# Two stretches per head pair, logits weighed apart from values, and table stores issued behind relus

## The chip, the cores and the metric

The kernel runs on one NeuronCore of one Trainium2 chip. A core has five instruction queues: PE (TensorE, matrix products; its weight loads are shown as PEld), DVE (VectorE), ACT (ScalarE), POOL (GpSimd) and SP (SyncE, which here only issues transfers). They run side by side and wait for each other through semaphores. The time is the device time of one execution, in microseconds (us). Three runs of the kernel before took 858.88, 858.96 and 869.34 us, so its time is the median, 858.96. The profile is of one further execution, which took 851.99 us.

## The reference

```python
# attention: B=8 batches, 8 heads, S=576 tokens, head size 64
scores = scale * np.matmul(q, k.transpose(0, 1, 3, 2))
cum = np.cumsum(np.maximum(s, 0.0), axis=-1)
bias = -(cum[:, :, :, None] - cum[:, :, None, :])
scores = np.where(causal, -1000000000.0, scores + np.minimum(bias, 0.0))
...
attn = attn / (np.sum(attn, axis=-1, keepdims=True) + 1e-09)
x = np.matmul(attn, v)                      # then heads side by side: 512 wide
# experts: 8 of them, 512 -> 1024 -> 512
logits = np.einsum('bsd,de->bse', x, w_gate)
local_gate = 1.0 / (1.0 + np.exp(-np.einsum('bsd,de->bse', x, w_local).squeeze(-1)))
# token by token: the argmax expert if s == 0 or local_gate < 0.5, else the expert of the token before
h = np.maximum(x[b, s] @ w1[e], 0.0)
out[b, s] = p[e] * (h @ w2[e])
```

All in float32, 4608 tokens.

## The kernel before

**Attention** runs over 32 pairs of heads, n = 0 to 32 with b, hp = n // 4, n % 4 (loop at L893). The bias splits into a factor for the query, which drops out in the division by the sum, and one for the key. So the values are multiplied once per batch by the keys' weights (`weigh`, L770), and the exponential of the plain scores is multiplied with them. `scores(n, u)` (L784) makes the transposed score tile u of a pair: PE multiplies kb by qb (L796), ACT takes the exponential into `e` (L798) and POOL zeroes what lies above the diagonal (L782). Tiles 0, 1 and 2 are 1024 wide and share two PSUM buffers `ps_s`; tile 3 is the 64-token tail `et` (L805, L806). `values(n, j0, j1)` (L816) multiplies the exponentials of a pair by the weighed values `vg` and the tail `vt` (L831, L834), and DVE divides by the sum into `xb`, the rows of x (L837 to L841). Beside its 64 values each row of `vg` carries the logits of the router for its token (from `value_logits`, L748, which multiplies vT by the gate's weights and copies the result into `va` and `vl`) and a column of ones, all weighed together at L775 and L778. So the rows and the logits of x come out of one product.

The order is written out by hand: each engine runs its instructions in the order of the program. Pair n's tiles 0 and 1 come first, then the first six value blocks of pair n - 1, then tiles 2 and 3, then the other three value blocks. `load_v(b + 1)` at the start of each batch issues vT, va and vl on SP; vl takes two transfers (L661). `load_qk(n + 4)` asks for q and k four pairs ahead. At n = 0 there is no earlier pair; instead `key_weights`, `value_logits(0)` and `weigh(0)` run. `constants` of the router, made on POOL after pair 3, ends in four pad stores to the table on SP (L178).

**The router** works on four groups of two batches each, with steps planned into later pairs (`plan`, L853). Its last step is `scatter`: `put` (L299) writes 128 half rows of `xb` to a DRAM table sorted by expert, with an indirect store issued by POOL, and before it a 1x1 memset of `gap`, also on POOL. 18 stores make a group. Those of group 2 that find no place before the end of attention are left in `rest`. Group 3 is ready only at the end.

**The experts** (`run`, L545) take the table in 30 units, in the order `DDDD`, four times `MDD`, twice `MDSS`. D is 256 rows of one expert, S is 128 rows, M is two pieces of 64 rows with an expert each. `fetch(u)` reads a unit's rows (five transfers for D and S, ten for M), `turn_x(u)` turns them (DVE), `layer1(u, c)` makes chunk c of the hidden layer on PE (L508, for M L499) and its relu on ACT (L510, L501), `layer2(u)` multiplies by the second matrix (L534), DVE scales it, and POOL stores the rows of the output (L539). `load(l)` brings the l-th pair of matrices, 2 MB each, into one of four places by l modulo 4; D and S have one load, M has two. Where a unit is followed by M the order is first layers of both, then second layers of both.

In unit 0 the last group's router steps come after chunks 1 and 5 (`todo`, L558). Once `rest` is issued, `load(1)`, `fetch(2)` and `fetch(3)` follow. After unit 0's first layer the kernel assigns rows to the later units, issues 18 stores of group 3 and 8 pad stores, and frees the space of `xb` for the fourth place of the weights, `w_last` (L602 to L612). Then `loads` asks for each further pair of matrices as soon as the unit four loads before is done.

Of the kernel before, what the change touches and what calls it, by code (L numbers as in the profile page):

```python
# [106 lines left out]
class Router:  # L107
# [186 lines left out]

    def scatter(self, g, c):
        st = self.g[g]
        self.put(st["x"][c // NJ][:, c % NJ].rearrange("p g f -> p (g f)"), st["idx"][:, c : c + 1])

    def put(self, src, idx):  # L299
        self.nc.gpsimd.memset(self.gap, 0.0)  # L300
        put = self.nc.gpsimd.indirect_dma_start(out=self.halves, in_=src, element_offset=0, in_offset=None,  # L301
                                                out_offset=bass.IndirectOffsetOnAxis(ap=idx, axis=0)).ins
        self.tc.declare_no_dep(put, group="puts", reason="no two rows of the table are the same")
        self.tc.add_to_no_dep_group("puts", put)

    def pads(self):
        v = self.nc.vector
        at = self.s("pad_at", [P, E])
        v.tensor_scalar(at, self.base, self.lane64, 2.0, Alu.add, Alu.mult)
        idx = self.t("pad_i", [P, E], I32)  # L310
        v.tensor_scalar(idx, at, self.half, None, Alu.add)
        return [lambda e=e: self.put(self.pad, idx[:, e : e + 1]) for e in range(E)]

# [85 lines left out]
class Experts:  # L399
    def __init__(self, ctx, tc, w1, w2, out, table, router):  # L400
# [11 lines left out]
        self.p_x = self.x_stack.enter_context(tc.tile_pool(name="p_x", bufs=2 * GB, side="right"))  # L412
        self.rest = []
        self.units = []
# [11 lines left out]
    def piece(self, u, i, row):  # L426
# [8 lines left out]
        else:  # L435
# [3 lines left out]
                                   skip_runtime_bounds_check_because="clamped when it was counted")  # L439

    def load(self, l, part=None):

        if l not in self.owner:
            return
        nc, u = self.nc, self.owner[l]
        if not part:
            pool = getattr(self, ("w_first", "w_rest", "w_rest", "w_last")[l % PLACES])
            self.ws[l] = pool.tile([P, DK, F], F32, name="w1b"), pool.tile([P, FK, D], F32, name="w2b")
            self.e = self.piece(u, self.units[u][2].index(l), 0)
        parts = 1 if part is None else 4  # L450
        for t, src in zip(self.ws[l], (self.w1, self.w2)):
            n = t.shape[1] // parts
            c = slice((part or 0) * n, (part or 0) * n + n)
            nc.sync.dma_start(t[:, c].rearrange("p c f -> p (c f)"),
                              src[bass.ds(self.e, 1), :, c].rearrange("o p c f -> (o p) (c f)"))
# [66 lines left out]

    def layer2(self, u):
        nc, mm = self.nc, self.nc.tensor.matmul
# [3 lines left out]
        for n in range(2 if kind == "D" else 1):  # L528
# [13 lines left out]
            self.tc.declare_no_dep(put, group="outs", reason="no two rows of the output are the same")  # L542
            self.tc.add_to_no_dep_group("outs", put)

    def run(self, recs, wend, out_of):  # L545
        tc, ctx, nc, router = self.tc, self.ctx, self.nc, self.router

        def pool(name, bufs, **kw):
# [7 lines left out]
        self.ps_y = pool("ps_y", 2, space=PSUM)  # L556
        last = NG - 1
        todo = {  # L558
            (0, 1): [lambda: router.product(last, self.ls, self.ps_m), lambda: router.codes(last),
                     lambda: router.turn1(last), lambda: router.turn2(last)],  # L560
            (0, 5): [lambda: router.ranks(last, self.ps_m), lambda: router.rows(last), lambda: router.gates(last, self.xb)],
        }

        def chunk(u, c):
            self.layer1(u, c)
            for f in todo.get((u, c), ()):
                f()

        kinds = [k for k, _, _ in self.units]
        for f in self.rest:  # L570
            f()
        self.load(1)
        self.fetch(2)
        self.turn_x(1)
        self.fetch(3)
        loaded = 2
        done = set()

        def loads():
            nonlocal loaded  # L580
            while loaded < PLACES or self.owner.get(loaded - PLACES, 99) in done:
                self.load(loaded)
                loaded += 1
                if loaded not in self.owner:
                    return

        order = []
        u = 0
# [7 lines left out]
        for what, u in order:  # L596
            if what == 1:
                for c in range(FK):
                    chunk(u, c)
                self.xT.pop(u)  # L600
                self.turn_h(u)
                if u == 0:  # L602
                    pads = router.pads()
                    router.assign_doubles()
                    router.assign_rest()
                    for c in range(NC):
                        router.scatter(last, c)
                    for f in pads:
                        f()
                    self.x_stack.close()  # L610
                    self.w_last = pool("w_last", 1, side="right")
                    loads()  # L612
                else:
                    self.turn_x(u + 1)
                    self.fetch(u + 3)
                if u == 1:
                    in_range(tc, recs, wend, router.over, out_of, self.ps_m)
            else:
                self.layer2(u)
                done.add(u)  # L620
                loads()


def attention(ctx, tc, q, k, vm, vt, vT, s, wbd_in, ident, recs, wend, router, experts):
# [17 lines left out]

    ins, vTs, es, xs = {}, {}, {}, {}
    heads = [slice(DH * h, DH * h + DH) for h in range(2)]
# [9 lines left out]
    def load_v(b):  # L654
        if b >= B:
            return
        vTs[b] = p_v.tile([P, HP, NB * P], F32, name="vTb")
        nc.sync.dma_start(vTs[b], vT[b])
        nc.sync.dma_start(va[:, :, :, :DH], vm[b])
        for h in range(2):  # L660
            nc.sync.dma_start(vl[heads[h], :, :DH], vt[b].rearrange("t (a h) d -> h t a d", h=2)[h])  # L661

# [8 lines left out]
    nc.vector.memset(ones, 1.0)  # L671
    va = once.tile([P, NF, H, VW - 1], F32, name="va")
    vl = once.tile([P, HP, VW - 1], F32, name="vl")
    vgs = [[once.tile([P, c, H, VW], F32, name=f"vg{g}{i}") for g, c in enumerate((G1, NF))] for i in range(2)]
    vts = [once.tile([P, HP, VW], F32, name=f"vt{i}") for i in range(2)]
    wbd = once.tile([P, HP, 2 * WR], F32, name="wbd")
    nc.sync.dma_start(wbd, wbd_in)
    load_v(0)
    for n in range(1, 4):
        load_qk(n)  # L680
    for t in (va, vl):
        nc.gpsimd.memset(t[..., VW - 2 : VW - 1], 1.0)
    for t in (*vgs[0], *vgs[1], *vts):
# [64 lines left out]
    def value_logits(b):  # L748
# [16 lines left out]
        nc.vector.transpose(tt.rearrange("p a h e -> p (a h e)"), pt.rearrange("p a e -> p (a e)"))  # L765
        nc.vector.tensor_copy(va[:, :, :, DH : DH + E + 1], tk[:, :, :, : E + 1])
        for h in range(2):
            nc.vector.tensor_copy(vl[heads[h], :, DH : DH + E + 1], tt[heads[h], :, h, : E + 1])

    def weigh(b):  # L770
        if b >= B:
            return
        for g, (n, wk) in enumerate(((G1, wk1), (NF, wk2))):
            shape = [P, n * H, VW - 1]
            nc.vector.tensor_tensor(vgs[b % 2][g].rearrange("p c h e -> p (c h) e")[:, :, : VW - 1],  # L775
                                    va.rearrange("p c h e -> p (c h) e")[:, : n * H],
                                    wk[:, b].rearrange("p c h -> p (c h)").unsqueeze(2).to_broadcast(shape), op=Alu.mult)
        nc.vector.tensor_tensor(vts[b % 2][:, :, : VW - 1], vl,  # L778
                                wkt[:, b].unsqueeze(2).to_broadcast([P, HP, VW - 1]), op=Alu.mult)

# [76 lines left out]
    for g in range(NG):  # L857
# [15 lines left out]
        for c in range(NC):  # L873
            if n + 4 + c // 2 <= NPAIR:
                plan(n + 4 + c // 2, 3, lambda g=g, c=c: router.scatter(g, c))
            else:
                experts.rest.append(lambda g=g, c=c: router.scatter(g, c))
    plan(3, 3, router.constants)
# [14 lines left out]
    for n in range(NPAIR + 1):  # L893
        b, hp = divmod(n, HP)
        if hp == 0 and n:
            load_v(b + 1)
        load_qk(n + 4)
        scores(n, 0)
        scores(n, 1)
        at(n, 0)  # L900
        if n == 0:
            key_weights()
        else:
            values(n - 1, 0, NJA)
        at(n, 1)
        scores(n, 2)
        scores(n, 3)
        at(n, 2)
        if n == 0:
            value_logits(0)  # L910
            weigh(0)
            load_v(1)
        else:
            values(n - 1, NJA, NJ)
        if hp == 1:
            value_logits(b + 1)
        if hp == 2:
            weigh(b + 1)
        at(n, 3)
# [39 lines left out]
def attention_general(ctx, tc, q, k, vm, vt, s, w_gate, w_local, cum_d, x_d, ident, lg):  # L959
# [24 lines left out]
    def load_batch(b):  # L984
# [8 lines left out]
        nc.sync.dma_start(vb, vm[b])  # L993
        nc.sync.dma_start(vl, vt[b])
        ins[b] = qb, kb, vb, vl
# [499 lines left out]
```

## Time and profile before

| | |
|---|---|
| median of three runs | 858.96 us |
| profiled execution | 851.99 us |
| its span, first to last instruction | 850.3 us |
| mean granted PE clock | 0.972 of full speed |

The busy time of each engine in five stretches of the span, from the trace (start and end in us):

```text
stretch           us     PE      DVE     ACT     POOL    PE clock
0.00:25.00        25.00  16.70   9.87    7.59    3.99    0.73
25.00:277.00      252.00 237.31  124.79  94.52   127.23  0.99
277.00:306.30     29.30  21.40   13.85   2.79    12.81   0.88
306.30:355.30     49.00  30.89   13.43   3.11    29.71   0.79
355.30:850.30     495.00 487.89  87.85   53.18   37.80   1.00
```

The first stretch is the start, the second is attention, the third is unit 0's first layer with the stores left from group 2, the fourth holds unit 0's second layer, unit 1's first layer and the 26 last stores, and the fifth is the rest of the experts. The largest groups of instructions are the two products of the experts; then come the value and the score products of attention. A group's row on the page gives line, engine, operation, what it writes and reads, the shapes, the count, then busy time and mean nanoseconds of one, then the engine's idle time just before it with what ended most of that:

```profile
L534 PE MATMUL yp<-w2b,hT 128*128 128x512 f32 (+1 forms) x704 | 266.4, 594 | 0.0
L508 PE MATMUL hp<-xT,w1b 128*128 128x256 f32 (+1 forms) x1152 | 232.9, 363 | 19.1 <-issue 18.1
L831 PE MATMUL po<-vg,e 128*64 128x75 f32 x3072 | 118.1, 231 | 6.7 <-POOL e L782 4.5
L796 PE MATMUL ps<-qb,kb 64*128 64x512 f32 (+4 forms) x640 | 105.7, 454 | 5.7 <-DMA qb<-in_q_dram 5.3
L301 POOL DMA_INDIRECT table<-xb,idx x72 | 71.2, 990 | 37.2 <-DVE be L341 14.0
```

### The profile page before, as it was taken

Reading aid. Unit: us, or ns where it says so; the run is one execution under the profiler, and the core shown is the slowest. Engines: PE = TensorE matmul, PEld = TensorE weight load, DVE = VectorE, ACT = ScalarE, POOL = GpSimd, SP = SyncE. Lnnn points to the kernel's source line nnn. Section 1 sums busy time; section 2 is a strip of 40 time slices with the busy share of each in tenths; the row PEclk is TensorE's granted clock in tenths of the full one; section 3 lists DMA queues with packets and bytes.
Section 4 is the critical chain, followed back from the end, with each engine's and each line's share of the span. In section 5 each row is a group of like instructions: output and inputs, shape, how many; then the busy total and the mean of one; then the engine's idle time right before and its main releaser. Section 6 shows DMA issues by size and latency. Waiting matters only on the chain.

```text
span 850.3 us, 16187 instructions
## 1 busy us (share of the span) xinstructions
PE 794.2 (93%) x6578; PEld 522.3 (61%) x6578; DVE 249.8 (29%) x692; ACT 161.2 (19%) x292; POOL 211.5 (25%) x491
## 2 busy tenths in 40 slices
PE   6989999999897793899999999999999999999996
PEld 3767777767676552675555646737646555683764
DVE  4434734754562372010320040040041022014000
ACT  2334434334343000110100201101101010010111
POOL 1353345656464648000010010000000001000000
PEclk7999999999999997799999999999999999999999
DMA  7657376488725595775149919937955974987910
GB/s 236 206 169 224 96 228 191 133 256 266 240 80 177 175 303 216 323 250 215 33 139 429 339 50 407 396 97 305 391 189 207 427 259 171 425 303 246 367 65 30
DMA packets 60901, 196.78 MB, mean 231 GB/s; under 512 B 16077, under 2 KB 36173, under 8 KB 52368
## 3 DMA queue, kind: packets, MB, share of 16 engines
q1 hardware_dynamic: 53936, 175.55, 59.0%
q0 software_dynamic: 6880, 20.10, 6.2%
q8 instruction: 54, 0.88, 0.4%
q14 instruction: 31, 0.25, 0.1%
HBM read 175.00 MB, written 21.14 MB: 231 GB/s over the span
## 4 chain that ended last, share of the span: by engine, by line
PE 82%; DMA 4%; issue 4%; POOL 2%; SPq 2%; another core or an unknown queue 2%; DVE 1%; ACT 1%; POOLq 0%; ACTq 0%; DVEq 0%
PE yp L534 31%; PE hp L508 26%; PE po L831 9%; PE ps L796 8%; PE hp L499 5%; DMA table<-xb,idx 3%; SPq L661 1%; DMA vTb<-in_vT_dram 1%; POOL table L301 1%; ACT e L798 1%; PE po L834 1%; PE pt L805 1%; POOL e L782 1%; PE vwp L756 1%
## 5 line engine op out<-in xcount | busy, mean ns | idle before, releaser
L534 PE MATMUL yp<-w2b,hT 128*128 128x512 f32 (+1 forms) x704 | 266.4, 594 | 0.0
L508 PE MATMUL hp<-xT,w1b 128*128 128x256 f32 (+1 forms) x1152 | 232.9, 363 | 19.1 <-issue 18.1
L508 PEld LDWEIGHTS hp<-xT,w1b 128*128 128x128 f32 x1152 | 202.8, 194 | 54.7 <-issue 28.9
L534 PEld LDWEIGHTS yp<-w2b,hT 128*128 128x128 f32 (+1 forms) x704 | 109.9, 175 | 148.4 <-issue 147.0
L539 POOL DMA_INDIRECT out_dram<-y,gi x38 | 37.3, 980 | 464.0 <-DVE y L537 438.6
L510 ACT ACTIVATE hT<-hp 128x256 f32<-128x256 f32 (+1 forms) x144 | 51.7, 360 | 469.0 <-PE hp L508 343.3
L831 PE MATMUL po<-vg,e 128*64 128x75 f32 x3072 | 118.1, 231 | 6.7 <-POOL e L782 4.5
L798 ACT ACTIVATE e<-ps 128x1024 f32<-128x1024 f32 x96 | 95.0, 1023 | 149.4 <-PE ps L796 137.3
L831 PEld LDWEIGHTS po<-vg,e 128*64 128x64 f32 x3072 | 107.1, 137 | 13.4 <-POOL e L782 4.8
L537 DVE TENSOR_SCALAR y<-yp,gi 128x512 f32<-128x512 f32 x38 | 28.3, 744 | 291.9 <-PE yp L534 285.4
L796 PE MATMUL ps<-qb,kb 64*128 64x512 f32 (+4 forms) x640 | 105.7, 454 | 5.7 <-DMA qb<-in_q_dram 5.3
L782 POOL TENSOR_SCALAR_AFFINE_SELECT e<-e 128x256 f32<-128x256 f32 x128 | 63.2, 514 | 108.9 <-ACT e L798 107.9
L796 PEld LDWEIGHTS ps<-qb,kb 64*128 64x128 f32 x640 | 58.1, 190 | 45.1 <-issue 36.0
L301 POOL DMA_INDIRECT table<-xb,idx x72 | 71.2, 990 | 37.2 <-DVE be L341 14.0
L519 DVE STREAM_TRANSPOSE hT<-hs 32x256 f32<-32x256 f32 x96 | 41.8, 436 | 115.2 <-ACT hs L501 113.9
L837 DVE RECIPROCAL recs<-po 128x12 f32<-128x12 f32 x64 | 13.5, 211 | 120.3 <-PE po L831 60.9
L499 PE MATMUL hp<-w1b,xT 128*64 128x512 f32 x192 | 42.5, 595 | 0.0
L839 DVE TENSOR_TENSOR xb<-po,recs 128x384 f32<-128x384 f32 x64 | 29.3, 458 | 9.8 <-DMA table<-xb,idx 7.7
L775 DVE TENSOR_TENSOR vg<-va,wk 128x1184 f32<-128x1184 f32 (+1 forms) x16 | 31.6, 2014 | 1.1 <-DMA va<-in_vm_dram 1.1
L499 PEld LDWEIGHTS hp<-w1b,xT 128*64 128x64 f32 x192 | 13.3, 137 | 25.8 <-issue 25.6
L484 DVE STREAM_TRANSPOSE xT<-xq 128x1024 f32<-128x1024 f32 (+1 forms) x24 | 24.4, 1015 | 0.2
L782 POOL TENSOR_SCALAR_AFFINE_SELECT et<-et 64x64 f32<-64x64 f32 x64 | 15.4, 240 | 16.5 <-DMA table<-xb,idx 14.8
(231 smaller groups left out, 227.7 us busy)
## 6 DMA issues: line engine op xcount, KB each, us to landing
w1b<-in_w_dram SPq DMA_DIRECT2D x29, 2048.0 KB
w2b<-in_w_dram SPq DMA_DIRECT2D x29, 2048.0 KB
vTb<-in_vT_dram SPq DMA_DIRECT2D x8, 1280.0 KB
kb<-in_k_dram SPq DMA_DIRECT2D x32, 288.0 KB
qb<-in_q_dram SPq DMA_DIRECT2D x32, 288.0 KB
va<-in_vm_dram SPq DMA_DIRECT2D x8, 1024.0 KB
xq<-table SPq DMA_DIRECT2D x56, 130.0 KB
w1b<-in_w_dram SPq DMA_DIRECT2D x4, 512.0 KB
```

The lines of the kernel that those rows point to most:

```text
L301: put = self.nc.gpsimd.indirect_dma_start(out=self.halves, in_=src, element_offset=0, in_offset=None, out_offset=bass.IndirectOffsetOnAxis ...
L499: mm(ps[d, :], lhsT=xT[:, k, d], rhs=self.ws[ls[i]][0][:, k, c * 512 : c * 512 + 512], start=(k == 0), stop=(k == DK - 1))
L508: mm(ps[:, :w], lhsT=self.ws[ls[0]][0][:, k, c * P : c * P + P], rhs=xT[:, k, :w], start=(k == 0), stop=(k == DK - 1))
L510: nc.scalar.activation(self.hT[u][:, c, :w], ps[:, :w], Act.Relu)
L519: self.nc.vector.transpose(hT[32 * a : 32 * a + 32, :, 32 * r : 32 * r + 32], hs[32 * r : 32 * r + 32].rearrange("p (c i) -> p c i", i=P)[ ...
L534: mm(ps[d, :], lhsT=hT[:, k, n * P + i * w : n * P + i * w + w], rhs=self.ws[ls[i]][1][:, k, :], start=(k == 0), stop=(k == FK - 1))
L539: put = nc.gpsimd.indirect_dma_start(out=self.out[:, :], out_offset=bass.IndirectOffsetOnAxis(ap=gi.bitcast(I32)[:, n, 0:1], axis=0), in_= ...
L775: nc.vector.tensor_tensor(vgs[b % 2][g].rearrange("p c h e -> p (c h) e")[:, :, : VW - 1], va.rearrange("p c h e -> p (c h) e")[:, : n * H ...
L782: nc.gpsimd.affine_select(out=ap, in_=ap, compare_op=Alu.is_ge, fill=0.0, base=0, pattern=n, channel_multiplier=-1)
L796: mm(ps[:, h, at : at + z - a], lhsT=kb[d, c * P : c * P + P], rhs=qb[d, a:z], start=True, stop=True)
L798: nc.scalar.activation(e, ps, Act.Exp, scale=scale)
L831: mm(po[d, j - j0, :], lhsT=weights_of(n, c, j, h), rhs=vg[:, c, 2 * hp + h, :], start=(c == 0), stop=(c == last))
```

## The change

In attention, the four score tiles of a pair run in one stretch (in the order 0, 1, 3, 2) and all its value blocks in another. The values `va` and `vl` are 64 wide and loaded by one transfer each, from a host layout of the tail in which each partition's row is contiguous. `load_v` is split from `load_vT`, both run a batch further ahead, and at the start v is asked for before the gate's weights and vT. `weigh` is split in two: `weigh_values` after pair 1 of a batch and `weigh_logits` after pair 3, straight from the turned logits; the column of the weights itself is written by a copy on ACT.

In the experts, the stores of the table (the 8 of `rest`, then 18 and 8 of the last group) are issued one behind each relu: a 1x1 copy from the relu's result into `gap` takes the place of the memset. The 8 go into unit 0, the 26 into units 1, 2 and 3 (one more after the first half of the second layers of units 1 and 2). The last group's first router steps move to chunk 2 of unit 0, its later ones to the middle of unit 0's second layer, the assignment of rows to units 1 and 2. `fetch(2)` and `fetch(3)` come after unit 0's first layer. The places of the loads change: 1 and 2 go to `w_rest`, 3 to `w_first`, 4 to `w_last`, which is opened when all stores are issued, at the end of unit 3's first layer; there `fetch(4)`, `fetch(5)` and loads 4, 5 and 6 follow. The first layer of unit 4 is the next one on PE.

```diff
     def put(self, src, idx, after=None):
-        self.nc.gpsimd.memset(self.gap, 0.0)
+        if after is None:
+            self.nc.gpsimd.memset(self.gap, 0.0)
+        else:
+            self.nc.gpsimd.tensor_copy(self.gap, after)
...
+    def place(l):
+        return ("w_first", "w_rest", "w_rest")[l] if l < 3 else ("w_first", "w_last", "w_rest", "w_rest")[(l - 3) % PLACES]
...
-            pool = getattr(self, ("w_first", "w_rest", "w_rest", "w_last")[l % PLACES])
+            pool = getattr(self, self.place(l))
...
+        def late_rows():
+            router.ranks(last, self.ps_m)
+            router.rows(last)
+            router.gates(last, self.xb)
+            self.puts += [lambda after, c=c: router.scatter(last, c, after) for c in range(NC)]
+            self.puts += router.pads()
         todo = {
-            (0, 1): [lambda: router.product(last, self.ls, self.ps_m), lambda: router.codes(last),
+            (0, 2): [lambda: router.product(last, self.ls, self.ps_m), lambda: router.codes(last),
                      lambda: router.turn1(last), lambda: router.turn2(last)],
-            (0, 5): [lambda: router.ranks(last, self.ps_m), lambda: router.rows(last), lambda: router.gates(last, self.xb)],
+            (0, "y"): [late_rows],
+            (1, 2): [router.assign_doubles],
+            (1, 5): [router.assign_rest],
+            (2, 5): [lambda: in_range(tc, recs, wend, router.over, out_of, self.ps_m)],
         }
...
         def loads():
-            while loaded < PLACES or self.owner.get(loaded - PLACES, 99) in done:
+            while loaded in self.owner:
+                if before.get(loaded) is not None and self.owner[before[loaded]] not in done:
+                    return
+                if self.place(loaded) == "w_last" and not freed:
+                    if self.puts or todo:
+                        return
+                    self.x_stack.close()
+                    self.w_last = pool("w_last", 1, side="right")
+                    freed = True
                 self.load(loaded)
                 loaded += 1
...
+        def between(u):
+            if self.puts:
+                self.puts.pop(0)(None)
+            at(u, "y")
...
                 for c in range(FK):
-                    chunk(u, c)
+                    self.layer1(u, c)
+                    at(u, c)
+                    if self.puts:
+                        self.puts.pop(0)(self.hT[u][0:1, c, 0:1])
+                    if u == 0 and fetched == 2 and not self.puts:
+                        fetches(3)
...
-                if u == 0:
-                    pads = router.pads()
-                    router.assign_doubles()
-                    router.assign_rest()
-                    for c in range(NC):
-                        router.scatter(last, c)
-                    for f in pads:
-                        f()
-                    self.x_stack.close()
-                    self.w_last = pool("w_last", 1, side="right")
+                if u == first - 1:
+                    fetches(first + 1)
                     loads()
...
     def load_v(b):
-        vTs[b] = p_v.tile([P, HP, NB * P], F32, name="vTb")
-        nc.sync.dma_start(vTs[b], vT[b])
-        nc.sync.dma_start(va[:, :, :, :DH], vm[b])
-        for h in range(2):
-            nc.sync.dma_start(vl[heads[h], :, :DH], vt[b].rearrange("t (a h) d -> h t a d", h=2)[h])
+        nc.sync.dma_start(va, vm[b])
+        nc.sync.dma_start(vl, vt[b])
+
+    def load_vT(b):
+        vTs[b] = p_v.tile([P, HP, NB * P], F32, name="vTb")
+        nc.sync.dma_start(vTs[b], vT[b])
...
     for n in range(NPAIR + 1):
         b, hp = divmod(n, HP)
-        if hp == 0 and n:
-            load_v(b + 1)
         load_qk(n + 4)
-        scores(n, 0)
-        scores(n, 1)
-        at(n, 0)
+        for u in (0, 1, 3, 2):
+            scores(n, u)
         if n == 0:
             key_weights()
-        else:
-            values(n - 1, 0, NJA)
+            weigh_values(0)
+            load_v(1)
+            value_logits(0)
+            load_vT(1)
+            weigh_logits(0)
+            continue
+        at(n, 0)
+        values(n - 1, 0, NJA)
         at(n, 1)
-        scores(n, 2)
-        scores(n, 3)
-        at(n, 2)
-        if n == 0:
-            value_logits(0)
-            weigh(0)
-            load_v(1)
-        else:
-            values(n - 1, NJA, NJ)
+        values(n - 1, NJA, NJ)
         if hp == 1:
+            weigh_values(b + 1)
+            load_v(b + 2)
+        if hp == 2:
             value_logits(b + 1)
-        if hp == 2:
-            weigh(b + 1)
+            load_vT(b + 2)
+        if hp == 3:
+            weigh_logits(b + 1)
         at(n, 3)
...
-        "vt": v[:, :, TS:].transpose(0, 2, 1, 3),
+        "vt": v[:, :, TS:].reshape(B, HP, 2, TL, DH).transpose(0, 2, 3, 1, 4).reshape(B, P, HP, DH),
```

## The prediction, made before the changed kernel ran

> **What bounds the kernel now.** I read the engine table first, then the chain of waits by lines, then that chain in order of time in the two places where TensorE (PE) is not full, then what the Pool engine does there.
>
> ```profile
> PE 794.2 (93%) x6578; PEld 522.3 (61%) x6578; DVE 249.8 (29%) x692; ACT 161.2 (19%) x292; POOL 211.5 (25%) x491
> PE 82%; DMA 4%; issue 4%; POOL 2%; SPq 2%; another core or an unknown queue 2%; DVE 1%; ACT 1%; POOLq 0%; ACTq 0%; DVEq 0%
> ```
>
> PE is busy for 93% of the span and no other engine for over 29%, so time can only come from PE's gaps and from the stretches where its clock is halved. From 356 us to the end PE has no gap, and no instruction there changes in kind or order, so I cost that at nothing. The first place is the start, in the chain's order of time (start, length, what):
>
> ```profile
> 4.37 8.71 SPq L661
> 13.08 0.04 issue
> 13.13 0.61 SPq L661
> ...
> 14.42 4.25 DMA qb<-in_q_dram
> 18.68 0.14 issue
> 18.81 3.89 PE ps L796 x12
> ```
>
> The SP queue spends 9.4 us on issuing the two small value-tail transfers of line 661; the q of pair 1, behind them, lands at 18.7. Its score products then take 3.89 us, against 1.98 for the same twelve at the full clock. The second place is the passage from attention to the experts:
>
> ```profile
> 271.51 19.78 another core or an unknown queue
> 291.29 0.02 issue
> 291.31 0.39 ACT hT L510
> ...
> 325.25 18.11 issue
> 343.35 11.76 PE hp L508 x40
> ...
> 410.43 7.02 PE hp L499 x32
> ```
>
> ScalarE's first relu (L510) runs at 291.31 though its products were done near 280.7; then PE itself stands for 18.1 us after three chunks of unit 1. Both ends coincide with bursts of table stores on POOL, in the timeline:
>
> ```profile
> 288.54 0.96 POOL L301 DMA_INDIRECT table<-xb,idx  x1 [0.21 <-issue]
> 289.50 0.09 POOL L300 MEMSET gap<- 1x1 f32 x1
> 289.81 0.96 POOL L301 DMA_INDIRECT table<-xb,idx  x1 [0.22 <-issue]
> 290.76 0.09 POOL L300 MEMSET gap<- 1x1 f32 x1
> 291.07 0.96 POOL L301 DMA_INDIRECT table<-xb,idx  x1 [0.22 <-issue]
> ```
>
> 12 stores run from 277.1 to 292.0 and 26 from 306.3 to 339.0, one each 1.27 us. The semaphore events of PE come late in both: the one for the products that end at 278.8 at 285.6, the one for unit 1's first chunk (ends near 322) only at 342.8. I read it so: **while stores are issued back to back, PE's completion signals are held**, relus wait, and when the three hp buffers are full PE stands. From the first product of unit 0 (278.75) to the first of unit 4 (410.43) is 131.7 us.
>
> **What the Trainium skill says.** "Perfetto Trace Analysis", section "Tensor Engine Instruction (MATMUL, LD_WEIGHTS)": the end shown for a matmul is estimated from its size, its semaphore follows later. The trace agrees in the extreme (21 us here). The same page, "DMA Instruction — SWDGE (GPSIMD)": the end shown is that of the descriptors, not of the data; here a store of 0.96 us lands 2.54 us after its start when alone. "TensorE: Matmul & The Clock Gate", "What's actually happening": an idle window of about 3.4 us halves the clock. Agrees: after the 18.1 us gap it was half until 349.2, 5.9 us, so 2.9 lost. "DMA: Bandwidth & Descriptors", "Queues, rings and completion order": SP's transfers share one row of rings, consumed in order; here weight transfers issued together landed one after another.
>
> **Part by part. Start.** The two transfers of L661 become one with whole rows per partition; I price its issue as the 0.4 to 0.7 of its neighbours. The data ahead of and with pair 1's q (s, two pairs of q and k, v, vT: 3.9 MB) needs about 9.3 us at the 420 GB/s of the weight loads, from about 4.5, so q lands near 14.2, not 18.7: −4.6, and −0.6 for less half clock. v now precedes vT, which costs the logits about 1 us, inside that estimate. Together −5.2 (−3 to −7).
>
> **vT ahead by a batch.** At 60.5 PE waits 2.3 us for vT, because SP stood at the pad stores of line 178, which need POOL's constants. vT of that batch is now issued some 40 us before: −2.3. The 8 to 12 us that line 661 took of SP in each later batch hid nothing but itself, since q and k come four pairs ahead: 0.
>
> **Order within a pair.** A steady pair takes 7.03 us, with PE full; each switch between score and value products shows a bubble of about 0.15. Six switches become five, but scores(2) needs a score buffer that the exp of scores(0) frees 2.26 us after the pair's start, where PE would be there at 2.24 plus a start-up: up to 0.1 of wait. Net 0.05 to 0.15 over 31 pairs; I take −2.5 (0 to −5).
>
> **v and logits apart.** Per batch DVE weighs 64 of 74 columns (3.95 us becomes an estimated 3.4), loses three copies (0.6), gains four small products (about 0.8); ACT gains three copies of some 0.2. DVE is busy 125 of 252 us there and ACT 95, and a batch lasts 28: hidden, 0; without that cover the new operations' 1.4 us a batch. On POOL the masks of the last score tile now queue behind the tail mask that waits for the landing of the previous stores (2.54, up to 6 to 8 under load). They are due 3.4 us into the next pair, so I take 0, bounded by −4 (the two waits of POOL's masks at 267 and 275 were 4.5 us) and +4.
>
> Attention: −5.2 −2.3 −2.5 = **−10.0** (−16 to −3).
>
> **Passage.** Pure work to unit 4: four first layers at 13.8, three second layers at 13.73, 1.3 for the router's products = 97.7. Before, 131.7 − 97.7 = 34 went into holds and half clock. Now each of 34 stores waits for a relu (1.72 us apart), and a 1x1 copy takes the place of the 0.09 memset. In attention two stores in a pair cost PE 0.1 to 0.25, so I take 0.1 a store: +3.5. No row shows a store every 1.72 us: the bounds are 0 and about 1 us each. The fetches of units 2 and 3 now follow the eight stores of unit 0, 18 us into it with some 6 us of SP, and are due at 27 and 55; the weights of unit 3 follow them and are due at 83: 0. The first of the 26 later stores must wait for those reads (about 27) and comes at 29: 0, a near miss that would only bunch some stores.
>
> **The new wait.** Of the 26 last stores the final one follows the last relu of unit 3. The buffers of the fourth weights, and the fetches of units 4 and 5, come only after it, and PE's next work is unit 4, which needs the first matrices of both its experts. Counted from PE's end of unit 3's first layer: relu, copy and store 1.5, landing 2.6; 15 transfers on SP ahead of the weights (ten for unit 4 at 6 us, five for unit 5 at 3.1, as at 297.4 to 300.5) = 13.2, register loads 0.6; the first weights landed 7.75 us after issue at 303.5, and each 2 MB more takes 5.0; unit 4 needs the third (w1, w2, w1): 13.8 + 7.75 + 10 = **31 us** (24 to 36), plus 2.9 of half clock. Behind PE's waiting product stand the second layers of units 3 and 4; nothing else can fill it. In the kernel before, these weights were requested after units 0 and 1.
>
> Passage: 97.7 + 3.5 + 31 + 2.9 = 135.1 against 131.7: **+3.4** (−4 to +9 with small holds, +34 with 1 us a store).
>
> **Sum.** −10.0 + 3.4 = −6.6 against the profiled execution's 851.99: 845.4. That execution was 7.0 under the median of 858.96 (858.88 and 869.34 are the others), so on the median: **852**.
>
> **The rivals.** (1) Likeliest: the hold goes and a wait for weights of the same size takes its place: 852, own range 842 to 865. (2) Slower: *stores still hold PE's signals though paced*. At 1.27 us busy of each 1.72, only 0.45 us is free between them; the late semaphores under bursts speak for it, the cheap pairs with two stores against. At 1 us each: +31 on 852, about 882. It passes 2% (876) with 24 us more than counted: 27.5 over 34 stores, so from 0.8 us a store. (3) Faster: attention gives its −16 and the weights come at the lower bound with no hold (−4 to −10 in the passage, if SP's fetches overlap the landing more than I count): 833 to 840. For it: all of attention's gaps are on PE's path. Against: full pairs leave only bubbles. (4) The new order saves no bubble, because scores(2) waits for the exp: −2.5 falls away, or a pair is 0.1 longer: 855 to 858, still no change.
>
> **Numbers.** Within 2% is about what a measurement of this kernel can't tell from no change. Rivals (1) and (4) have 0.34 and 0.10, so same 0.44; (2) with a late mask chain in attention 0.31; (3) 0.25. Range 832 to 884: it takes in (3) and (2), with both unknown costs at their bounds.
>
> **What would show it.** Right: pair 1's scores near 14, no wait for vT at 60, pairs of 6.9 to 7.0; relus of units 0 to 3 evenly 1.72 apart; one PE gap of about 31 us before the first product of line 499's kind, released by a weight transfer. Wrong: PE gaps inside the first layers of units 0 to 3 with PE semaphores late (2), a gap under 20 (3), or score products that wait for an exp in each pair (4).

## The result, and the profile after

The changed kernel takes 862.01 us (20 runs, 855.59 to 864.30), the kernel before 860.95 in the same sessions (20 runs, 856.08 to 869.34). The ratio is 1.0005, with a 95% interval of 0.9984 to 1.0026: no change. The forecast was 6.6 us less. The first profile after has a span of 859.4 us, 9.1 over the first one before. A second pair of profiles, both taken on one chip, stands at 858.1 after and 855.4 before, and its 2.7 us agree with the times of that set (ratio 1.0029, 1.0005 to 1.0053), so I read sizes from that pair where I can.

| us | before | after | before, again | after, again |
|---|---|---|---|---|
| first scores of pair 11 | 99.4 | 92.0 | 101.6 | 94.1 |
| first scores of pair 31 | 263.5 | 271.1 | 269.2 | 271.8 |
| first product of unit 0 | 278.7 | 286.0 | 284.7 | 286.3 |
| from there to the end of unit 4's first layer | 138.7 | 140.7 | 138.0 | 139.1 |
| from there to PE's last product | 425.7 | 425.7 | 425.7 | 425.7 |

At pair 11, where both kernels have made the logits of the same batches, attention is 7.6 us ahead (in the first profiles 7.4), of the 8.3 forecast to there (5.2, 2.3 and a third of 2.5). From there to pair 31 it loses 10.2 (15.0). Pairs 11, 19 and 27 lose 5.9 of that (8.5), pairs 21, 22 and 29 together 6.7 (8.2), and the others gain 2.4 (1.7). The passage to the experts is about even, and what follows is equal to a tenth.

The busy table and the chain by engines, from the page of the changed kernel, hardly differ from those before:

```profile
PE 795.6 (93%) x6578; PEld 523.9 (61%) x6578; DVE 249.9 (29%) x700; ACT 164.6 (19%) x316; POOL 213.9 (25%) x489
PE 82%; DMA 5%; DVE 3%; issue 3%; POOL 3%; SPq 1%; ACT 1%; another core or an unknown queue 1%; POOLq 0%; DVEq 0%; ACTq 0%
```

PE is as busy as before, so its idle time was exchanged, not removed. The waits of PE (engine, line, waited for: us in total, times, longest) say for what:

```profile
PE hp L507 <- DMA w1b<-in_w_dram: 29.1, 2, 21.4
PE ps L851 <- ACT e L853: 9.1, 7, 3.2
PE po L886 <- issue: 5.3, 13, 1.1
PE pt L860 <- DVE tt L806: 3.5, 2, 1.8
PE vwp L797 <- DMA vTb<-in_vT_dram: 3.5, 1, 3.5
```

The first row is the forecast wait for the weights of unit 4, in two parts. The second and the fourth had no counterpart before: score tile 2 waits for the exponential of tile 0, and the tail product for VectorE. The kernel before waited 4.5 us for POOL's masks at the end of attention instead, and that wait is absent here. At the start the chain in order of time (start, length, what) runs over vT, which now comes behind v:

```profile
4.11 9.47 DMA vTb<-in_vT_dram
13.58 0.14 issue
13.71 1.93 PE vwp L797 x32
...
16.07 3.52 PE ps L851 x12
```

Pair 1 starts at 16.0, not 18.8. In the passage, the timeline (start, length, engine, line, operation, tiles, count, and in brackets the idle time before it with its releaser) shows relus that come evenly, and one hole:

```profile
289.41 0.38 ACT L518 ACTIVATE hT<-hp 128x256 f32<-128x256 f32 x1 [13.71 <-PE hp L516]
291.13 0.38 ACT L518 ACTIVATE hT<-hp 128x256 f32<-128x256 f32 x1 [1.34 <-PE hp L516]
292.86 0.38 ACT L518 ACTIVATE hT<-hp 128x256 f32<-128x256 f32 x1 [1.34 <-PE hp L516]
...
372.37 13.98 PE L516 MATMUL hp<-xT,w1b 128*128 128x256 f32 x64
407.71 1.94 PE L507 MATMUL hp<-w1b,xT 128*64 128x512 f32 x2 [21.36 <-DMA w1b<-in_w_dram]
417.36 9.33 PE L507 MATMUL hp<-w1b,xT 128*64 128x512 f32 x30 [7.71 <-DMA w1b<-in_w_dram]
```

A store behind each relu costs PE nothing, units 0 to 3 run with one wait of PE, of 0.8 us, and then PE stands 29.1 us and does unit 4's first layer in 11.3 instead of 7.0.

Two pairs of attention show the new waits. Pair 11 (timeline of the changed kernel):

```profile
92.03 2.05 PE L851 MATMUL ps<-qb,kb 64*128 64x512 f32 x12
...
93.91 0.46 DVE L247 TENSOR_TENSOR_SCAN incl<-seg,hot 128x144 f32<-128x144 f32 x1
...
94.86 0.70 DVE L804 STREAM_TRANSPOSE tk<-vwp 128x512 f32<-128x512 f32 x1
95.49 0.27 DVE L806 STREAM_TRANSPOSE tt<-vwt 128x128 f32<-128x128 f32 x1
95.82 0.33 PE L860 MATMUL pt<-qb,kb 64*64 64x64 f32 x4 [1.74 <-DVE tt L806]
...
98.37 4.64 PE L886 MATMUL po<-vg,e 128*64 128x75 f32 x96
```

The logits' products of batch 3 moved to the pair of the router's second turn (L231 to L247). VectorE turns the logits (L804, L806) only after that, and their single PSUM buffer is the one the tail product needs, now 2 us after the pair's start instead of nearly 5. After the wait the granted clock is at half from 97.66 to 101.07, and the value products take 4.64 us instead of 3.3. The pair takes 11.2 us, against 7.9 before. And pair 29, which took 9.0 us before and takes 12.1:

```profile
250.10 1.00 POOL L305 DMA_INDIRECT table<-xb,idx  x1 [0.15 <-issue]
251.35 2.05 PE L851 MATMUL ps<-qb,kb 64*128 64x512 f32 x12
...
253.94 0.96 POOL L305 DMA_INDIRECT table<-xb,idx  x1 [0.22 <-issue]
...
256.14 1.94 ACT L853 ACTIVATE e<-ps 128x1024 f32<-128x1024 f32 x2 [7.12 <-PE pt L860]
257.22 1.27 PE L851 MATMUL ps<-qb,kb 64*128 64x320 f32 x8 [2.54 <-ACT e L853]
```

The same pair in the kernel before:

```profile
247.46 2.05 PE L796 MATMUL ps<-qb,kb 64*128 64x512 f32 x12
...
248.11 1.00 POOL L301 DMA_INDIRECT table<-xb,idx  x1 [0.16 <-POOL gap L300]
248.70 1.94 ACT L798 ACTIVATE e<-ps 128x1024 f32<-128x1024 f32 x2 [2.15 <-PE ps L796]
...
249.44 1.74 PE L831 MATMUL po<-vg,e 128*64 128x75 f32 x43
```

Both have four stores, and the difference is where they fall. In the new order POOL has made its masks 1.4 us before the next pair's first scores, so the burst begins 1.25 us ahead of them; in the old order the last mask ends 0.35 us after they begin, and the burst starts at 0.65. The first exponential follows the first scores by 4.79 us instead of 1.24. In the kernel before it follows by 1.24 in every pair from 9 on but one (pair 26); in the changed kernel it is late in seven. Tile 2, which needs the buffer of tile 0, then waits with nothing of PE's in between. In the old order value products stand there, and they do cover a delay: in pair 22 of the run g0 below, which has the old order, the exponential is 1.55 us late and the pair takes 7.34 us, against 7.05 and 7.22 in the two traces of the kernel before. Which of the two, the earlier burst or the missing cover, costs more was not tested apart.

### The profile page after: what moved, and what is told of

It is laid out like the page before. It is cut to its first block, busy times and chain, and to the rows that moved or that the text cites. A ratio compares the mean times of both kernels' runs of the same rounds, so it can differ in the third digit from the quotient of the medians.

```text
span 859.4 us, 16248 instructions
## 1 busy us (share of the span) xinstructions
PE 795.6 (93%) x6578; PEld 523.9 (61%) x6578; DVE 249.9 (29%) x700; ACT 164.6 (19%) x316; POOL 213.9 (25%) x489
## 4 chain that ended last, share of the span: by engine, by line
PE 82%; DMA 5%; DVE 3%; issue 3%; POOL 3%; SPq 1%; ACT 1%; another core or an unknown queue 1%; POOLq 0%; DVEq 0%; ACTq 0%
PE yp L542 31%; PE hp L516 24%; PE po L886 10%; PE ps L851 9%; PE hp L507 5%; DMA table<-xb,idx 2%; DMA w1b<-in_w_dram 2%; POOL table L305 2%; DMA vTb<-in_vT_dram 1%; ACT e L853 1%; PE pt L860 1%; DVE vg L815 1%; PE po L889 1%; PE vwp L797 1%
## 5 line engine op out<-in xcount | busy, mean ns | idle before, releaser
L516 PE MATMUL hp<-xT,w1b 128*128 128x256 f32 (+1 forms) x1152 | 227.4, 358 | 0.0
L516 PEld LDWEIGHTS hp<-xT,w1b 128*128 128x128 f32 x1152 | 199.7, 191 | 33.0 <-issue 10.3
L886 PEld LDWEIGHTS po<-vg,e 128*64 128x64 f32 x3072 | 109.6, 141 | 14.7 <-issue 13.1
L507 PE MATMUL hp<-w1b,xT 128*64 128x512 f32 x192 | 46.7, 626 | 29.1 <-DMA w1b<-in_w_dram 29.1
L815 DVE TENSOR_TENSOR vg<-va,wk 128x1024 f32<-128x1024 f32 (+1 forms) x16 | 27.8, 1779 | 0.0
L509 ACT ACTIVATE hs<-hp 128x512 f32<-128x512 f32 x12 | 7.2, 597 | 69.7 <-PE hp L507 69.7
```

Source lines behind the costliest of these rows:

```text
L507: mm(ps[d, :], lhsT=xT[:, k, d], rhs=self.ws[ls[i]][0][:, k, c * 512 : c * 512 + 512], start=(k == 0), stop=(k == DK - 1))
L516: mm(ps[:, :w], lhsT=self.ws[ls[0]][0][:, k, c * P : c * P + P], rhs=xT[:, k, :w], start=(k == 0), stop=(k == DK - 1))
L815: nc.vector.tensor_tensor(to[:, :, :DH], va.rearrange("p c h e -> p (c h) e")[:, : n * H], w.to_broadcast([P, n * H, DH]), op=Alu.mult)
L886: mm(po[d, j - j0, :], lhsT=weights_of(n, c, j, h), rhs=vg[:, c, 2 * hp + h, :], start=(c == 0), stop=(c == last))
```

## The experiments

Times are compared through the ratio to the kernel before in the same set. The sets differ: in the first (x1 to x4) the kernel before took 841.2 us, in the others 857 to 861.

**First set: parts of the change undone.** x1 puts the value blocks back between the score tiles, the other parts stay:

```diff
-        for u in (0, 1, 3, 2):
+        for u in (0, 1) if n else (0, 1, 3, 2):
             scores(n, u)
...
         at(n, 1)
+        scores(n, 2)
+        scores(n, 3)
         values(n - 1, NJA, NJ)
```

> The changed kernel with one thing put back: tiles 2 and 3 of the scores come between the two parts of the value blocks again. Theory A (in one stretch tile 2 waits for the exponential of tile 0, and the tail product for the turn of the logits, with nothing of PE's between, so each delay of ScalarE or VectorE, or of PE's signals while table stores are issued, lies on PE's path): the 16 us lost between pairs 10 and 31 mostly come back, 846 to 853. Theory B (the loss comes from the moved logits, the order of POOL's masks and the stores themselves, whatever the order of PE): 858 to 864.

Measured 847.86, ratio 1.0073 (1.0049 to 1.0096): neither, and slower than its neighbours. x2 moves the second turn behind the logits:

```diff
-        plan(n + 2, 1, lambda g=g: router.turn2(g))
-        plan(n + 3, 0, lambda g=g: router.ranks(g, ps_m))
-        plan(n + 3, 1, lambda g=g: router.rows(g))
+        plan(n + 2, 3, lambda g=g: router.turn2(g))
+        plan(n + 3, 1, lambda g=g: router.ranks(g, ps_m))
+        plan(n + 3, 3, lambda g=g: router.rows(g))
```

> The changed kernel with the router's second turn after all value blocks of its pair instead of after the first six, so VectorE turns the logits first; ranks and rows follow half a pair later. Theory A: the tail product's wait for the single buffer of the logits and the half clock behind it go in the three pairs that have both, 3 to 4 us each: 850 to 855. Rival: the wait only moves to the products of the ranks or to the rows, no change: 860 to 864.

Measured 839.73, ratio 0.9971 (0.9947 to 0.9994). Against the ratios of the changed kernel elsewhere (1.0005 and 1.0029; it was not run in this set) that is 3 to 5 us less, where 7 were expected at the least. Its trace shows the wait gone, the clock stays full, and pair 11 takes 8.0 us:

```profile
91.52 2.05 PE L851 MATMUL ps<-qb,kb 64*128 64x512 f32 x12
...
92.35 0.27 DVE L806 STREAM_TRANSPOSE tt<-vwt 128x128 f32<-128x128 f32 x1
...
93.49 0.33 PE L860 MATMUL pt<-qb,kb 64*64 64x64 f32 x4
```

The tail product follows the scores at once. x3 joins the attention of the kernel before to the experts of the changed one:

> The attention of the kernel before with the experts and stores of the changed one. Theory A: the passage costs 2 us more than before, as in the two profiles (140.6 against 138.7 us from the first product of unit 0 to the end of unit 4's first layer): 861 to 865. Theory B (the timed runs of the kernel before are 9 us over its profiled one because its passage varies, and the paced stores end that): 853 to 858.

Measured 856.24, ratio 1.0180 (1.0123 to 1.0238), in time 15 us slower: neither. x4 issues a pair's stores ahead of the masks of tile 2:

```diff
         for u in (0, 1, 3, 2):
             scores(n, u)
+            if u == 3:
+                at(n, "p")
...
-                plan(n + 4 + c // 2, 3, lambda g=g, c=c: router.scatter(g, c))
+                plan(n + 4 + c // 2, "p", lambda g=g, c=c: router.scatter(g, c))
```

> The changed kernel with the stores of a pair in attention issued ahead of the masks of tile 2 instead of behind them, so that they run under the value blocks and not under the next pair's first scores. Theory A (stores hold PE's signal for the first scores, the exponential starts 0.6 to 3 us late, and tile 2 waits for it): 5 to 8 us come back, 854 to 858. Rival (the masks of tile 2 come late and the values wait for them, or the hold only falls on another signal): 862 to 870.

Measured 841.62, ratio 1.0009 (0.9982 to 1.0035).

What follows from this set was seen only beside the next. In its traces I find no store that delays a signal of PE: pair 13, which has two stores beside its first scores in x2 as in the changed kernel, takes 6.95 us here and 7.6 to 7.7 in the other sets, and pair 29 with its four takes 6.95 against 12.0 to 13.3. And here the forecast gain of attention is there, and more: with the order before (x3) attention ends at 280.4, in x2 and x4, each with one edit, at 265.4 and 266.7 (one trace each). I infer that the bursts of the kernel before cost less too (no trace of it was taken there). They can hardly have cost nothing: x3 waits 29.2 us for the weights, yet lost only 15. x1 is the slowest of x1, x2 and x4, and the only one without the one stretch, but in the traces the 5 us by which its attention ends later than that of x2 lie in pairs 25 and 26, where ScalarE stands behind a step of the router. That the order is no loss where no signal is held is therefore a hint only.

**Second set: the same again, one half alone, and the wait for weights.**

> The kernel before, unchanged, once more with a trace. Its first profiled execution had 278.7 us of attention and a passage (first product of unit 0 to the end of unit 4's first layer) of 138.7. Theory C (that profile was an odd one; as a rule the bursts of stores hold PE for less and the passage is 122 to 130): 122 to 130 here. Theory A (the passage is 137 to 141 in every execution): 137 to 141.

> The changed kernel, unchanged, on the same chip as the experiments beside it: ratio 0.998 to 1.003 to the kernel before. Theory C (attention gained about what was forecast, and its first profile was an odd one): attention ends at 266 to 272, not at 286. Theory A (pairs with stores or router steps lose 16 us in every execution): 282 to 288.

The kernel before: 858.37, passage 138.0. The changed one: 859.60, ratio 1.0029 (1.0005 to 1.0053), attention to 286.3. Theory C, that the first profiles were odd ones, fell in both. The next has the changed attention and the old experts with their bursts:

> The attention of the changed kernel with the experts and stores of the kernel before, the complement of the earlier mixture that was 1.8% slower. Theory C (attention gains 10 to 15 us, the passage of the changed experts costs that much more than before): ratio 0.982 to 0.989. Theory A (attention loses, the passage is about even): 0.998 to 1.008.

Measured 859.51, ratio 1.0033 (1.0009 to 1.0058): attention alone gains nothing. The passage is 11.0 us shorter than in the kernel before (127.0), but attention ends at 298.0 instead of 284.7. Its last pair is instructive, in the timeline of the value products:

```profile
282.77 0.38 PE L847 MATMUL po<-vg,e 128*64 128x75 f32 x5 [0.37 <-issue]
...
288.51 0.53 PE L847 MATMUL po<-vg,e 128*64 128x75 f32 x4 [0.90 <-issue]
...
293.51 0.52 PE L847 MATMUL po<-vg,e 128*64 128x75 f32 x3 [1.14 <-issue]
295.62 0.41 PE L847 MATMUL po<-vg,e 128*64 128x75 f32 x2 [1.59 <-issue]
```

A burst of 12 stores runs from 280.05 on, when the last value products begin (in the kernel before, again, from 282.6, near their end), and PE does one to six small products at a time with pauses up to 1.6 us, for which the profile shows nothing awaited ("issue"). From pair 31 to unit 0 it takes 24.9 us, with stores behind relus 14.5. So a burst not only delays signals; it also seems to keep PE short of instructions where those are short. e3 is the changed kernel with the places of the loads, the last stores and with them the fetches of units 4 and 5 moved:

```diff
-        return ("w_first", "w_rest", "w_rest")[l] if l < 3 else ("w_first", "w_last", "w_rest", "w_rest")[(l - 3) % PLACES]
+        return ("w_first", "w_rest", "w_rest")[l] if l < 3 else ("w_first", "w_rest", "w_rest", "w_last")[(l - 3) % PLACES]
...
-            if self.puts:
+            for _ in range(min(5, len(self.puts))):
                 self.puts.pop(0)(None)
...
-                if u == first - 1:
-                    assert not self.puts
-                    fetches(first + 1)
-                    loads()
...
                 done.add(u)
+                if u == first - 2:
+                    assert not self.puts
+                    fetches(first + 1)
                 loads()
```

> The changed kernel with two edits in the experts: loads 4 and 5 go to the places that units 1 and 2 leave and load 6 to the one that waits for the stores; and five stores instead of one run in the second layers of units 1 and 2, so that all are out, and units 4 and 5 fetched, before unit 3. If the wait for the first weights of unit 4 is a plain 29 us on PE's path with half a clock behind it, it goes and nothing takes its place: 30 to 33 us less than the changed kernel, ratio 0.962 to 0.967. Rival (the bursts of five hold PE's signals, or the rows of unit 4 come as late as its weights did): 0.985 to 1.0.

Measured 834.88, ratio 0.9734 (0.9666 to 0.9801). Passage 116.3 instead of 139.1; the first layer of unit 4 now reads

```profile
384.75 1.07 PE L507 MATMUL hp<-w1b,xT 128*64 128x512 f32 x2
392.46 8.79 PE L507 MATMUL hp<-w1b,xT 128*64 128x512 f32 x30 [6.63 <-DMA w1b<-in_w_dram]
```

The 21.4 us are gone, 6.6 remain, because load 5 still queues behind the fetches of units 4 and 5. That is the term the expectation missed. The five stores in a second layer, where PE waits for no other engine, cost nothing.

**Third set: order and turn on top of e3.** The attention of e3 is that of the changed kernel. f1, f2 and f3 add the edits of x1, of x2, and of x2 and x4 to it.

> The kernel with early weights once more, as the base of the three beside it, all of which have its experts. Ratio 0.970 to 0.977 to the kernel before; attention as in the changed kernel, 283 to 288 us where the stores hold PE's signals, 266 to 272 where they don't.

> The base with tiles 2 and 3 of the scores between the two parts of the value blocks again. If the lost slack of the one stretch is what turned the forecast gain of attention into nothing, it is 8 to 14 us below the base where the stores hold signals, and even (each pair 0.08 longer, the tail's wait gone) where they don't. Rival (the order is not the cause): 2 to 5 us above the base everywhere.

> The base with the router's second turn behind the turn of the logits. Theory: the wait of the tail product for the logits' buffer goes in pairs 11, 19 and 27, with the half clock behind it: 4 to 7 us below the base, those pairs take 8.0 us instead of 9 to 12. Rival (the wait moves): within 1 us of it.

> As the one before, and the stores of a pair ahead of the masks of tile 2, so that they fall under the value blocks. Theory (a store that runs while the first scores end delays the exponential, and tile 2 with it): pairs 13, 14, 16, 21 and 29 lose their 0.6 to 6 us, 6 to 12 below the one before where stores hold signals. Rival (the hold falls on another signal or the masks come late): within 2 of it.

| | us | ratio to before (interval) | attention ends |
|---|---|---|---|
| f0, base | 839.01 | 0.9765 (0.9684 to 0.9845) | 286.3 |
| f1, values between the scores | 826.75 | 0.9610 (0.9535 to 0.9685) | 278.4 |
| f2, second turn late | 828.85 | 0.9646 (0.9559 to 0.9734) | 280.5 |
| f3, second turn late, stores early | 839.10 | 0.9759 (0.9678 to 0.9839) | 286.8 |

Here the old order saves 12.3 us, and the late turn alone 10.2; with four runs of each I take either as some 5 us uncertain. In the traces attention ends 7.9 and 5.8 us sooner (the traced execution of f1 was the slowest of its four). They are not two separate gains, since in the old order the tail product also comes later than the turn. PE's waits between 20 and 300 us show what each left (in these kernels the scores are L850, their exponential L852, the values L885). Base:

```profile
PE ps L850 <- ACT e L852: 7.9, 7, 2.5
PE po L885 <- issue: 4.7, 13, 0.5
PE pt L859 <- DVE tt L805: 3.7, 2, 2.0
```

Values between the scores (f1): the wait for VectorE is absent, that for the exponential down to one, and the wait for POOL's masks at the end is back, as in the kernel before.

```profile
PE po L885 <- POOL e L836: 4.3, 2, 2.8
PE po L885 <- issue: 3.1, 9, 0.4
...
PE ps L850 <- ACT e L852: 1.7, 1, 1.7
```

Second turn late (f2): the wait for VectorE is absent, the other still there.

```profile
PE ps L850 <- ACT e L852: 9.9, 7, 3.3
...
PE po L885 <- issue: 4.0, 9, 1.1
```

Stores early as well (f3):

```profile
PE po L885 <- issue: 12.3, 26, 1.9
PE ps L850 <- ACT e L852: 2.6, 4, 1.2
```

The stores moved off the first scores and onto the value products, and 7.3 us of waiting for the exponential became 8.3 us of waiting for instructions: the rival of that experiment. Of the two places tried for the stores in a pair of the changed order, neither was cheap.

**Fourth set: the old attention against the parts.** All three have the experts of e3; the first has the attention of the kernel before.

> The attention of the kernel before (old order, old loads of v) with the experts of the base with early weights. If the start and vT give the 7.5 us forecast and the order alone costs 12, it lies between: 6 to 9 us above the interleaved kernel beside it, 3 to 6 below the base. Rival (the early loads of v and the split weighing give nothing as a time): within 2 us of the interleaved kernel.

> The interleaved kernel with early weights once more, on the same chip as its neighbours: ratio 0.957 to 0.968, 9 to 14 us below the base where stores hold PE's signals.

> The base with early weights (attention of the changed kernel) once more as the common reference: ratio 0.970 to 0.978.

Measured: old attention 840.61 (0.9763, 0.9696 to 0.9831), values between the scores 828.23 (0.9601, 0.9534 to 0.9667), base 838.16 (0.9729, 0.9665 to 0.9793). The old attention lies 12.4 us above the interleaved one, more than the 6 to 9 expected, and 2.4 above the base, not below it. So the loads of v and vT and the split weighing are worth about 12 us as a time, the order in two stretches takes 9.9 of that away, and the 2.4 left to attention as changed are not clear of the scatter of four runs. In the traces attention ends at 286.2, 281.0 and 284.3, so the two differences are only 5.2 and 3.3 there; the traced execution of the interleaved kernel was the slowest of its four, those of the other two the fastest.

The interleaved kernel with early weights beats both: 826.75 and 828.23 us in two sets, 3.9 and 4.0% below the kernel before.

## Why the prediction was wrong

**Direction of the sum.** −6.6 us was forecast and +0.4 measured (by the ratio). Two of its three main terms held.

**Start and vT: right.** By pair 3, where both kernels have the logits of batch 1 behind them, 4.4 us were gained (forecast 5.2; pair 1 began at 16.0 rather than 14.2, since vT landed at 13.6 behind v and the logits ahead of the pair wait for it). From pair 4 to pair 7 the gain grew by 2.6 (vT, forecast 2.3). As a time, all but the order is worth 12.4 (5.2 in the traces).

**"Order within a pair", −2.5, is the step that failed, and with it the 0 under "v and logits apart"** for POOL's masks (bound +4) and for the logits that moved. In an undisturbed pair the term is right: 6.93 to 6.96 us instead of 7.00 to 7.04, about 2.3 over 31 pairs. But I took from such a pair that scores(2) would wait at most 0.1 us for the exponential of tile 0, and asked only whether each engine had time enough in a batch (VectorE 125 of 252 us). The question was what stands between a product and its consumer. In the old order 1.7 us of value products did, in the new one nothing, so every late exponential and every late turn of the logits is on PE's path. They were late for two reasons. The masks that end sooner let the bursts of stores begin ahead of the next first scores, and bursts delayed PE's signals, as the passage had shown; a pair with two stores lost 0.1 to 0.25 us before and loses 0.57 (pair 16) to 0.74 (pair 13) now. And the logits were moved into the pair of the router's second turn, while their one PSUM buffer is needed 2 us into the next pair. In place of −2.5 and 0 the two cost +9.9 to +12.3 (3.3 and 7.9 in the traces); pairs 11 to 31 lost 10.2 us in the second pair of profiles. Undoing the meeting of turn and logits alone (f2) brought back 10.2 with the order kept, so the shares of the two are not told apart.

**Passage: right in kind and nearly in size.** The wait for the weights was 29.1 against 31, the half clock behind it 4.2 against 2.9, and PE waited 0.8 us in units 0 to 3, against 3.5 for holds by 34 paced stores. In all +2.0 and +1.1 in the two pairs of profiles, against +3.4.

**The rivals.** Rival 2's mechanism was the right one in the wrong place: paced stores in the experts held nothing, but unpaced ones in attention did, because there the change moved them onto the first scores and took away the cover. Of rival 4 (the new order saves nothing, because tile 2 waits for the exponential) the mechanism was right too and its size, 3 to 6 us, too small.

**The median.** The first three runs of the kernel before gave 858.96, twenty gave 860.95, so 2 of the 10 us between 852 and 862 were the base.

What stays open: why stores hold PE at all, and why they did not in the first set, whose kernels ran on a chip that showed the hold in the fourth. Where they held nothing, attention gained more than forecast; so the cost of the order is shown for the later sets only.

## What to carry to other kernels

Before two stages that alternate on the busiest engine are merged into one stretch each, list for every product what must come back from another engine before it, and how much other work stood between; the mean load of that engine says nothing about it. List also what those engines will start earlier, and what it then falls on. A stall on the path that is traded for another of equal length is no gain, but a plain wait for a transfer was easy to remove here: moving three loads, the fetches of two units and eight stores was worth 24.7 us. Of the places tried for a burst of stores, the one that cost nothing was under long instructions of the busiest engine that wait for nobody, here the second layers.

## What the runs showed of the hardware

- While POOL issued indirect stores of 0.96 us back to back, one each 1.27 us, value products (0.035 us each at full pace) ran in groups of one to six, 0.15 to 1.6 us apart (the last pair of the attention-only kernel). The experts' products (0.22 us each in a first layer, 0.43 in a second) ran at full pace beside a store every 1.72 us, and those of the second layers beside bursts of five.
- Four such stores, beginning 1.25 us ahead of the first scores, delayed the exponential behind them by 3.55 us (pair 29), and beginning 0.65 us after them not at all. In one set of runs they delayed nothing, on a chip where they did in another; the kernel before took 841.2 us in that set and 860.7 in the other.
- One wait of PE of 1.74 us, with sparse products behind it, came with a halved clock for 3.4 us (pair 11); without the wait (x2) the clock stayed full there.
